# Batch 0's tokens loaded flat and its attention in two token halves: a cross-attention and snake-MLP kernel on one Trainium2 core, its first 312 steps in a new order

## The chip, the core and the metric

The kernel runs on one core of a Trainium2 chip. TensorE (PE) multiplies a stationary operand (loaded by LDWEIGHTS, PEld in the profile) with a moving one into the eight banks of PSUM; VectorE (DVE), ScalarE (ACT) and GpSimd (POOL) do the elementwise work, and SyncE (SP), ACT and POOL issue transfers (DMA). The metric is the device time of one execution in microseconds (us); less is better.

## The reference, cut to what matters

```python
# x: (8, 8, 512, 64), state: (8, 8, 32, 64); batch, head, token or slot, width
scores = scale * x @ state^T;   a = softmax(scores);    xread = a @ state
scores2 = scale * state @ x^T;  a2 = softmax(scores2);  sread = a2 @ x
rows = concat([xread, sread], axis=2)      # heads side by side: (8 * 544, 512)
h = rows @ w_in                            # w_in: (512, 2048)
g = h + sin(alpha * h) ** 2 / (alpha + 1e-9)
out = g @ w_out                            # w_out: (2048, 512), out: (4352, 512)
```

## The kernel before, in words

Work goes by tiles t = 0 to 7, one for each batch (its 512 tokens), and t = 8, the 256 state rows of all batches. For a batch the steps are, by the names of the methods:

- x is loaded (`lx`: a POOL transfer that casts to bf16; batch 0 instead `lq`: four transfers of SP, two heads each, in fp32), packed and cast (`pk`, for batch 0 `xq` on ACT), transposed (`xt`, for batch 0 `xtq`, on TensorE; from batch 2 on `td`, a transposing DMA of SP), and copied out of PSUM (`xc`).
- `sc`, `ex`, `rs`, `rr`, `nm`: scores against the transposed state `stT`, exponentials, sums over 32 slots, reciprocals, normalized weights A. The index after the batch is the group of four heads; each call covers all 512 tokens.
- A is transposed (`at` and `ac` on TensorE and a copy for batch 0; `ad`, a transposing DMA, for the others).
- `m` multiplies state with a quarter (slice s) of w_in, `me` evicts it to M. So h = A times M, and xread is never formed.
- `h` or `hg`: one block f of 128 of the 2048 columns of h, two products of 512 columns. `si`: sin(alpha h) on ACT. `sq`: the square, on the engine that the step names (A, V or G). `gt`: g, transposed, on VectorE.
- `o.t.st.f0.f1`: products f0 to f1 - 1 of the 16 that make the output tile of 128 rows; `oc` evicts it, `os` stores it.
- `w`, `cs`, `rc`, `xs`: sread of a batch, for tile 8. For batch 0 they come some 10 us after the last store of its tile.

The state of batches 0 and 1 comes early by `l_s01`, `s01_c`, `s01_t`, `s01_k`; that of the other batches by `l_st`, `st_t`, `st_c`. `li` and `lo` load a quarter of w_in and w_out each, 1 MB of fp32 cast to 0.5 MB, on POOL's queue. `l_alpha`, `al_t`, `al_c`, `inva` prepare alpha. `exp_table` and `sin_table` load ACT's function tables. `warm_up.n.cols.bank` is n products on zeros, whose result nobody reads.

Nothing is scheduled at run time: `ORDER` is a list of steps written out by hand or by a planner, and each engine executes its share of it strictly in this order; a step waits for its inputs and for its PSUM bank (the number in the step), and what stands behind it on its engine waits with it.

```python
    for step in ORDER:
        name, *args = step.split(".")
        getattr(steps, name)(*(int(a) if a.isdigit() else a for a in args))
```

Of the kernel before, what the change touches and what calls it, by code (L numbers as in the profile page):

```python
# [33 lines left out]
me.1.1.1.A warm_up.2.128.2 gt.0.2 si.0.0 warm_up.2.128.2 warm_up.2.128.6 warm_up.2.128.3
warm_up.2.128.2 warm_up.2.128.6 me.0.1.0.A gt.0.1 sq.0.0.G m.0.2.3.2 si.0.3 m.1.2.5.6 hg.0.4.0.7
me.0.2.0.V me.0.2.1.A hg.0.4.1 sq.0.3.G hg.0.6.0.4 me.1.2.1.V hg.0.6.1 si.0.4 hg.0.7.0.3 hg.0.11.0.2
me.1.2.0.V si.0.6 hg.0.7.1 sq.0.4.G hg.0.5.0.6 gt.0.0 hg.0.5.1 si.0.7 hg.0.11.1 hg.0.8.0.5 hg.0.8.1
sq.0.6.A gt.0.3 sq.0.7.G o.0.3.0.2.0 si.0.5 gt.0.4 o.0.3.2.3 o.0.0.0.2.1 si.0.11 o.0.0.2.3 gt.0.6
sq.0.5.G o.0.0.3.4 o.0.2.0.1.7 si.0.8 o.0.3.3.5 sq.0.11.A gt.0.7 hg.0.9.0.4 sq.0.8.G o.0.2.1.2
gt.0.5 o.0.2.2.4 hg.0.9.1 gt.0.11 o.0.0.4.5 hg.0.10.0.3 si.0.9 o.0.2.4.5 gt.0.8 o.0.0.5.6 o.0.3.5.6  # L40
sq.0.9.A o.0.3.6.8 pk.1.0.V hg.0.10.1 xt.1.1.6 pk.1.1.V si.0.10 gt.0.9 xt.1.0.2 xc.1.1.0.A sq.0.10.G
o.0.2.5.6 xc.1.1.1.V xc.1.0.0.A o.0.0.6.7 xc.1.0.1.V o.0.0.7.8 o.0.2.6.7 sc.1.1.5 gt.0.10 sc.1.0.4
m.0.3.6.2 ex.1.0 o.0.2.7.8 me.0.3.0.V o.0.1.0.3.3 me.0.3.1.V o.0.1.3.6 hg.0.13.0.6 o.0.1.6.7 ex.1.1
rs.1.0 hg.0.13.1 m.1.3.2.4 si.0.13 o.0.1.7.8 rr.1.0 rs.1.1 nm.1.0.0.4.G o.0.1.8.9 hg.0.12.0.5
o.0.3.8.9 rr.1.1 hg.0.12.1 me.1.3.0.V o.0.0.8.9 nm.1.1.0.4.G o.0.1.9.10 o.0.0.9.10 me.1.3.1.V
# [618 lines left out]
```

The softmax here doesn't subtract the row's maximum and nothing guards it: scores larger than these inputs give would overflow.

## Time and profile before

| | |
|---|---|
| median of 3 runs | 221.26 us (220.95 to 222.09) |
| the profiled execution: span from first to last instruction | 221.2 us; the profile gives no time beside it |
| PE, DVE, ACT, POOL busy | 97%, 73%, 78%, 48% of the span |
| instructions of PE and its share in the chain that ended last | 1619, 93% |
| warm-up products (line 303) | 66, 9.9 us, the last at 19.2 us |
| DMA queues: q0 (POOL), q1 (SP) | 8.13 MB and 15.08 MB, 26.1% of 16 engines each |
| first sine, first product of `o`, product of step o.1.1.0.1 | 16.52, 22.55, 45.85 us |

A line of the timeline is: start, length, engine, line of the code, operation, what it writes and reads, and how many are merged; in brackets the idle time of the engine before it and what ended it. The chain is followed back from the last instruction: at each step to what released it. "Busy" for PE counts matmuls that wait in its pipeline too, so neighbouring matmuls overlap in it.

### The profile page before, as it was taken

How to read it: one execution, taken by the hardware profiler on the slowest of the kernel's cores; microseconds unless marked ns; L12 is line 12 of the kernel's file. 1: busy time of each engine (PE TensorE's matmuls, PEld its weight loads, DVE VectorE, ACT ScalarE, POOL GpSimd, SP SyncE). 2: the span in 40 equal slices, each digit the busy share in tenths (PEclk: the TensorE clock that was granted, in tenths of full speed). 3: DMA queues.
4: the chain of work that ended last, by engine and by line, in shares of the span. 5: the costliest groups of instructions: out<-in, count | busy, mean ns of one | idle time of the engine just before them, and what ended most of it. 6: DMA issues, size and time to landing. Idle time of an engine off the chain costs nothing.

```text
span 221.2 us, 4330 instructions
## 1 busy us (share of the span) xinstructions
PE 215.7 (97%) x1619; PEld 106.0 (48%) x1619; DVE 162.4 (73%) x286; ACT 173.5 (78%) x297; POOL 107.1 (48%) x115
## 2 busy tenths in 40 slices
PE   7999999999999999999999999999999999999994
PEld 3664454444444444444454444445445555665452
DVE  3468986999678979988888778889766988571201
ACT  3589878998899979998996999798857897685111
POOL 6866626595388728934863377363501072121000
PEclk9999999999999999999999999999999999999999
DMA  6999995953549518375325437380220211012042
GB/s 172 198 206 204 205 203 87 174 199 73 119 127 158 96 50 150 44 190 61 81 41 125 126 95 94 108 117 17 47 99 0 98 47 47 0 50 95 1 142 96
DMA packets 38052, 23.48 MB, mean 106 GB/s; under 512 B 20992, under 2 KB 33680, under 8 KB 38032
## 3 DMA queue, kind: packets, MB, share of 16 engines
q0 software_dynamic: 11648, 8.13, 26.1%
q1 hardware_dynamic: 26128, 15.08, 26.1%
q8 instruction: 12, 0.20, 0.4%
q14 instruction: 8, 0.07, 0.1%
q10 hardware_dynamic: 256, 0.01, 0.1%
HBM read 17.44 MB, written 8.91 MB: 119 GB/s over the span
## 4 chain that ended last, share of the span: by engine, by line
PE 93%; ACT 3%; DMA 2%; SPq 0%; issue 0%
PE o_ps L587 54%; PE h_ps L537 22%; PE m_ps L488 4%; PE h_ps L543 3%; PE h_ps L552 3%; DMA x<-in_x_dram 2%; PE s_ps L399 2%; PE warm_ps L303 2%; PE w_ps L450 2%; PE w_ps L461 1%; PE x_ps L361 1%; ACT L226 1%; ACT s L560 1%; ACT M L496 1%; PE x_ps L376 0%; PE st_ps L333 0%
## 5 line engine op out<-in xcount | busy, mean ns | idle before, releaser
L587 PE MATMUL o_ps<-w_out_sb,gT 128*128 128x512 bf16 (+2 forms) x560 | 137.7, 373 | 0.0
L576 DVE SCALAR_TENSOR_TENSOR gT<-s,inva_sb,h_ps 128x512 bf16<-128x512 bf16 (+1 forms) x144 | 96.6, 714 | 18.8 <-POOL s L201 9.6
L201 POOL TENSOR_TENSOR s<-s 128x512 bf16<-128x512 bf16 (+1 forms) x76 | 76.7, 1021 | 65.9 <-ACT s L560 62.4
L560 ACT ACTIVATE s<-h_ps,alpha_sb 128x512 bf16<-128x512 f32 (+1 forms) x144 | 88.8, 671 | 10.5 <-PE h_ps L543 4.3
L587 PEld LDWEIGHTS <-gT 128*128 128x128 bf16 x560 | 52.3, 98 | 60.3 <-issue 5.0
L537 PE MATMUL h_ps<-AT,M 128*128 128x512 bf16 x224 | 60.8, 379 | 0.0
L537 PEld LDWEIGHTS <-M 128*128 128x128 bf16 x224 | 21.7, 98 | 25.9 <-issue 0.4
L569 ACT ACTIVATE s<-s 128x512 bf16<-128x512 bf16 (+1 forms) x53 | 31.4, 595 | 0.8
L201 POOL TENSOR_TENSOR A<-E,rR 128x512 bf16<-128x512 bf16 x16 | 16.6, 1048 | 25.7 <-ACT o_sb L595 12.7
L595 ACT COPY o_sb<-o_ps 128x512 f32<-128x512 f32 (+2 forms) x24 | 13.7, 571 | 16.6 <-PE o_ps L587 16.5
L496 ACT CAST M<-m_ps 128x512 bf16<-128x512 f32 x35 | 18.6, 594 | 8.2 <-PE m_ps L488 8.1
L496 DVE CAST M<-m_ps 128x512 bf16<-128x512 f32 x29 | 18.9, 679 | 2.5 <-PE m_ps L488 2.1
L595 DVE COPY o_sb<-o_ps 128x512 f32<-128x512 f32 x11 | 7.6, 691 | 13.0 <-PE o_ps L587 12.9
L303 PE MATMUL warm_ps<-warm 128*128 128x128 bf16 (+3 forms) x66 | 9.9, 295 | 1.4 <-DVE warm L209 1.2
L410 DVE TENSOR_REDUCE R<-E 128x16 f32<-128x512 bf16 x16 | 10.4, 658 | 1.1 <-ACT E L406 0.9
L201 DVE TENSOR_TENSOR s<-s 128x512 bf16<-128x512 bf16 (+1 forms) x15 | 6.2, 415 | 6.8 <-ACT s L560 6.7
L488 PE MATMUL m_ps<-w_in_sb,stT 64*32 64x512 bf16 x256 | 10.2, 382 | 0.0
L468 DVE RECIPROCAL rC<-w_ps 128x128 f32<-128x128 f32 x8 | 7.6, 948 | 3.2 <-PE w_ps L461 3.2
L406 ACT ACTIVATE E<-s_ps 128x512 bf16<-128x512 f32 x16 | 8.8, 601 | 1.4 <-PE s_ps L399 1.3
L552 PE MATMUL h_ps<-AT,M 128*128 128x512 bf16 x32 | 9.4, 380 | 0.4 <-ACT M L496 0.4
L543 PE MATMUL h_ps<-xs_all,w_in_sb 128*128 128x256 bf16 x64 | 9.1, 273 | 0.0
L560 ACT ACT_TABLE_LOAD x5 | 6.4, 1283 | 2.2 <-PE h_ps L537 1.1
(56 smaller groups left out, 104.3 us busy)
## 6 DMA issues: line engine op xcount, KB each, us to landing
out_dram<-o_sb SPq DMA_DIRECT2D x33, 256.0 KB, 2.3
xnat<-in_x_dram POOLq DMA_DIRECT2D x7, 512.0 KB, 7.7
w_in_sb<-in_moe_w_in_dram POOLq DMA_DIRECT2D x4, 512.0 KB, 10.3
w_out_sb<-in_moe_w_out_dram POOLq DMA_DIRECT2D x4, 512.0 KB, 16.3
x<-in_x_dram SPq DMA_DIRECT2D x4, 256.0 KB, 4.3
st_nat<-in_state_dram POOLq DMA_DIRECT2D x1, 256.0 KB, 5.7
out_dram<-o_sb SPq DMA_DIRECT2D x1, 192.0 KB, 1.9
s<-in_state_dram SPq DMA_DIRECT2D x1, 128.0 KB, 2.1
```

What stands on the lines that cost most here:

```text
L201: {"V": k.nc.vector, "G": k.nc.gpsimd}[eng].tensor_tensor(out, a, b, ALU.mult)
L303: k.nc.tensor.matmul(wp[:, :cols], k.warm[:, 0:k.P], k.warm[:, :cols], start=True, stop=True)
L488: k.nc.tensor.matmul(k.t["m", b, s + n, g][o0:o0 + k.Ns, :], k.stT[k.half(r), b * k.G + g, c0:c0 + k.Ns], k.w_in_sb[k.half(r), 2 * g + h, ...
L496: k.copy(eng)(k.t["M", b][:, g, s * k.FW:(s + 1) * k.FW], k.t["m", b, s, g][:])
L537: k.nc.tensor.matmul(hp[:, :n], k.t["M", t][:, g, fs], k.t["AT", t][:, g, :], start=(g == 0), stop=(g == k.G - 1),)
L543: k.nc.tensor.matmul(hp[:, :n], k.w_in_sb[:, q, fs], k.xs_all[:, q].rearrange("p b j -> p (b j)"), start=(q == 0), stop=(q == k.Q - 1),)
L552: k.nc.tensor.matmul(k.t["h", t, f][:], k.t["M", t][:, g, f * k.P:(f + 1) * k.P], k.t["AT", t][:, g, :], start=(g == 0), stop=(g == k.G - 1),)
L560: k.nc.scalar.activation(s[:, :n], k.t["h", t, f][:, :n], ACT.Sin, scale=k.alpha_sb[:, f:f + 1])
L569: k.nc.scalar.activation(s2[:, :n], s[:, :n], ACT.Square)
L576: k.nc.vector.scalar_tensor_tensor(gT[:, :n], k.t["s2", t, f][:, :n], k.inva_sb[:, f:f + 1], k.t["h", t, f][:, :n], ALU.mult, ALU.add,)
L587: k.nc.tensor.matmul(k.t["o", t, st, half][:, cols], k.t["gT", t, f][:, rows], k.w_out_sb[:, f, cols], start=(f == 0), stop=(f == k.FT - 1),)
L595: k.copy(eng)(o_sb[:, cols], k.t["o", t, st, half][:, cols])
```

## The change

- Batch 0's x is read flat: partition p holds 32 successive tokens of one head (2048 values). Columns j = 0 to 15 of the 32 come by two SP transfers in fp32 (`lf`) and two casts on ACT (`xn`), j = 16 to 31 by one casting POOL transfer (`lfb`). `lq`, `xq` and `xtq` go.
- `xth` transposes four pairs of columns j at a time, `xc` puts the result into `xT0` with the tokens of a half together. `sc0`, `ex0`, `rs0`, `rr0`, `nm`, `at0`, `ac0` do the attention of 256 tokens at a time. `sc0` takes one head at a time (32 moving columns, 64 rows), against a copy of the state, `st0T` (`s01_0`).
- `hh` does a block of h of tile 0 in two halves of 256 columns.
- The token-major x that `w.0` needs is now made by `td.0`, a transposing DMA of `xT0`; `w.0` has 32 products of 32 columns instead of 16 of 64.
- `os` of tile 0 writes its rows in the new token order, still 2 KB each.
- The first 312 steps have a new order: x of batch 0, then `li`, `lo`, `lx.1` and `l_st` in another order on POOL's queue, fewer warm-ups (13 products), other banks. From `o.1.1.0.1` on the steps are the same in the same order; only bank numbers differ.

The head of the list, old and new:

```diff
-touch_x l_s01 consts touch lq.0.S ident_ l_alpha lq.1.S zero.0 warm_up.7.512.3 exp_table lq.2.S
-zero.1 identf.V lq.3.S s01_c.G l_st li.0 xq.0.A s01_t.4 li.1 xtq.0.5 warm_up.1.384.3 xq.1.A
-s01_k.1.V s01_k.0.A li.2 xtq.1.6 warm_up.2.448.3 xc.0.0.0.V xq.2.A xc.0.0.1.V lo.0 al_t.7 xq.3.A
-xtq.2.0 warm_up.1.384.3 al_c inva sc.0.0.1 lo.1 xc.0.1.0.A warm_up.1.256.3 xtq.3.2 warm_up.2.128.3
-ex.0.0 warm_up.2.128.4 lx.1.0.1 warm_up.2.128.5 xc.0.1.1.V warm_up.2.128.6 warm_up.2.128.7 rs.0.0
-sc.0.1.0 li.3 st_t.0.3 ex.0.1 rr.0.0 st_t.1.4 lo.2 st_c.0.0.V st_c.0.1.A warm_up.2.128.5
-warm_up.2.128.6 warm_up.2.128.1 st_c.1.0.A rs.0.1 warm_up.2.128.2 warm_up.2.128.7 nm.0.0.0.4.G
-warm_up.2.128.0 warm_up.2.128.5 st_c.1.1.A warm_up.2.128.3 warm_up.2.128.6 warm_up.2.128.1 rr.0.1
-warm_up.2.128.2 sin_table warm_up.2.128.7 warm_up.2.128.0 nm.0.1.0.4.G at.0.0.5 warm_up.2.128.3
-ac.0.0.V m.0.0.6.4 m.1.0.1.2 lo.3 at.0.1.7 me.0.0.0.V me.0.0.1.A warm_up.2.128.0 warm_up.2.128.3
-me.1.0.1.A ac.0.1.V hg.0.2.0.5 me.1.0.0.V hg.0.1.0.4 hg.0.2.1 hg.0.1.1 hg.0.0.0.0 lx.2.0.1 si.0.2
-hg.0.0.1 m.1.1.6.3 si.0.1 m.0.1.7.2 hg.0.3.0.1 me.0.1.1.A sq.0.2.V hg.0.3.1 sq.0.1.G me.1.1.0.V
-me.1.1.1.A warm_up.2.128.2 gt.0.2 si.0.0 warm_up.2.128.2 warm_up.2.128.6 warm_up.2.128.3
-warm_up.2.128.2 warm_up.2.128.6 me.0.1.0.A gt.0.1 sq.0.0.G m.0.2.3.2 si.0.3 m.1.2.5.6 hg.0.4.0.7
-me.0.2.0.V me.0.2.1.A hg.0.4.1 sq.0.3.G hg.0.6.0.4 me.1.2.1.V hg.0.6.1 si.0.4 hg.0.7.0.3 hg.0.11.0.2
-me.1.2.0.V si.0.6 hg.0.7.1 sq.0.4.G hg.0.5.0.6 gt.0.0 hg.0.5.1 si.0.7 hg.0.11.1 hg.0.8.0.5 hg.0.8.1
-sq.0.6.A gt.0.3 sq.0.7.G o.0.3.0.2.0 si.0.5 gt.0.4 o.0.3.2.3 o.0.0.0.2.1 si.0.11 o.0.0.2.3 gt.0.6
-sq.0.5.G o.0.0.3.4 o.0.2.0.1.7 si.0.8 o.0.3.3.5 sq.0.11.A gt.0.7 hg.0.9.0.4 sq.0.8.G o.0.2.1.2
-gt.0.5 o.0.2.2.4 hg.0.9.1 gt.0.11 o.0.0.4.5 hg.0.10.0.3 si.0.9 o.0.2.4.5 gt.0.8 o.0.0.5.6 o.0.3.5.6
-sq.0.9.A o.0.3.6.8 pk.1.0.V hg.0.10.1 xt.1.1.6 pk.1.1.V si.0.10 gt.0.9 xt.1.0.2 xc.1.1.0.A sq.0.10.G
-o.0.2.5.6 xc.1.1.1.V xc.1.0.0.A o.0.0.6.7 xc.1.0.1.V o.0.0.7.8 o.0.2.6.7 sc.1.1.5 gt.0.10 sc.1.0.4
-m.0.3.6.2 ex.1.0 o.0.2.7.8 me.0.3.0.V o.0.1.0.3.3 me.0.3.1.V o.0.1.3.6 hg.0.13.0.6 o.0.1.6.7 ex.1.1
-rs.1.0 hg.0.13.1 m.1.3.2.4 si.0.13 o.0.1.7.8 rr.1.0 rs.1.1 nm.1.0.0.4.G o.0.1.8.9 hg.0.12.0.5
-o.0.3.8.9 rr.1.1 hg.0.12.1 me.1.3.0.V o.0.0.8.9 nm.1.1.0.4.G o.0.1.9.10 o.0.0.9.10 me.1.3.1.V
-si.0.12 o.0.0.10.11 o.0.3.9.11 sq.0.13.G ad.1 hg.0.15.0.2 sq.0.12.A o.0.1.10.12 hg.0.15.1 gt.0.12
-o.0.2.8.10 si.0.15 o.0.2.10.11 gt.0.13 o.0.0.11.12 hg.0.14.0.4 sq.0.15.A hg.0.14.1 o.0.3.11.13
...
+l_s01 ident_ touch_x consts lf.0.S touch zero.0 lfb lf.1.S l_alpha identf.V li.0 zero.1 exp_table
+li.1 s01_c.V warm_up.4.512.6 s01_t.0 lo.0 xn.0.A al_t.1 s01_0.V lx.1.0.1 s01_k.1.V s01_k.0.A
+warm_up.1.224.7 xth.0.0.2 xn.1.A al_c inva li.2 xc.0.0.A warm_up.1.352.0 xth.0.1.3 xth.0.2.4 lo.1
+xc.0.1.A xth.0.3.5 xc.0.2.V l_st sc0.0.6.7 xc.0.3.A ex0.0.0 warm_up.1.352.4 sc0.1.0.1 ex0.0.1 rs0.0
+ex0.1.0 ex0.1.1 sin_table rr0.0 warm_up.5.512.6 m.1.0.2.3 rs0.1 nm.0.0.0.2.G m.0.0.4.5 nm.0.1.0.2.G
+rr0.1 nm.0.0.2.4.V nm.0.1.2.4.G warm_up.1.512.1 at0.0.6 me.0.0.0.A m.0.1.7.0 li.3 ac0.0.V me.0.0.1.A
+at0.1.1 m.1.1.4.6 me.0.1.1.A ac0.1.V lo.2 hh.0.0.0.5 me.0.1.0.V me.1.0.1.A hh.0.0.1 hh.0.1.0.1
+hh.0.1.1 lo.3 me.1.0.0.V si.0.0 hh.0.2.0.0 hh.0.2.1 si.0.1 me.1.1.0.V hh.0.3.0.7 sq.0.0.G hh.0.3.1
+hh.0.4.0.3 si.0.2 me.1.1.1.V hh.0.4.1 hh.0.5.0.2 hh.0.5.1 si.0.3 sq.0.1.V sq.0.2.G gt.0.0 hh.0.6.0.4
+si.0.4 hh.0.6.1 gt.0.1 hh.0.7.0.6 si.0.5 sq.0.3.G hh.0.7.1 o.0.0.0.1.5 si.0.6 gt.0.2 xt.1.1.1
+sq.0.4.G si.0.7 gt.0.3 o.0.0.1.2 xt.1.0.0 xc.1.1.0.A xc.1.1.1.V sq.0.5.G sq.0.6.A o.0.1.0.1.7 gt.0.4
+sc.1.1.1 xc.1.0.0.A o.0.1.1.2 xc.1.0.1.V o.0.0.2.3 sq.0.7.G ex.1.1 o.0.2.0.1.3 gt.0.5 sc.1.0.0
+o.0.2.1.2 o.0.1.2.3 gt.0.6 o.0.3.0.1.2 o.0.3.1.2 o.0.2.2.3 gt.0.7 o.0.3.2.3 lx.2.0.1 o.0.0.3.4
+ex.1.0 m.0.2.4.1 pk.1.0.V o.0.1.3.4 pk.1.1.V me.0.2.0.A m.1.2.6.0 me.0.2.1.V o.0.2.3.4 me.1.2.1.A
+o.0.3.3.4 o.0.0.4.5 rs.1.0 me.1.2.0.A hh.0.8.0.4 hh.0.8.1 rs.1.1 st_t.0.1 si.0.8 rr.1.0 st_t.1.0
+rr.1.1 st_c.0.0.V nm.1.0.0.4.G hh.0.9.0.6 st_c.0.1.V hh.0.9.1 o.0.1.4.5 o.0.2.4.5 st_c.1.0.V
+nm.1.1.0.4.G si.0.9 hh.0.10.0.1 hh.0.10.1 sq.0.8.V o.0.3.4.5 st_c.1.1.A o.0.0.5.6 sq.0.9.V o.0.1.5.6
+si.0.10 ad.1 gt.0.8 o.0.2.5.6 hh.0.11.0.0 hh.0.11.1 gt.0.9 o.0.3.5.6 sq.0.10.G si.0.11 o.0.0.6.7
+o.0.1.6.7 o.0.2.6.7 m.0.3.4.6 sq.0.11.A gt.0.10 o.0.3.6.7 o.0.0.7.8 me.0.3.0.A o.0.1.7.8 gt.0.11
+o.0.2.7.8 me.0.3.1.A o.0.3.7.8 m.1.3.1.4 hh.0.12.0.0 me.1.3.0.A me.1.3.1.V hh.0.12.1 hh.0.13.0.6
...
```

The new and changed functions:

```diff
-    def lq(k, q, eng):
...
+    def flat(k):
+
+        return k.x[0].rearrange("h (b j) d -> (h b) j d", j=32)
+    def flat_sb(k):
+        return k.new(0, "xf", k.const, [k.P, 32, k.D], BF16)
+    def lf(k, part, eng):
+        k.t["xa", part] = k.const.tile([k.P, 8, k.D], FP32, name=f"xa_{part}")
         {"A": k.nc.scalar, "S": k.nc.sync}[eng].dma_start(
+            k.t["xa", part][:], k.flat()[:, 8 * part:8 * part + 8, :]
+        )
+    def lfb(k):
+        k.nc.gpsimd.dma_start(k.flat_sb()[:, 16:32, :], k.flat()[:, 16:32, :])
+    def xn(k, part, eng):
+        k.copy(eng)(k.flat_sb()[:, 8 * part:8 * part + 8, :], k.t["xa", part][:])
...
+    def xth(k, b, part, bank):
+        tp = k.t["xth", b, part] = k.ps(bank, [k.P, 4, k.P], BF16, "x_ps")
+        for m in range(4):
+            j = 8 * part + 2 * m
+            k.nc.tensor.transpose(
+                tp[:, m, :], k.flat_sb()[:, j:j + 2, :].rearrange("p j d -> p (j d)"), k.ident[:]
+            )
+    def xT0(k):
+
+        return k.new(0, "xT0", k.const, [k.P, 2, k.H, 8, 16], BF16)
...
     def td(k, b):
+        if b == 0:
+            xp = k.new(0, "xp", k.xppool, [k.P, 2, k.H, 2, k.D], BF16)
+            k.nc.sync.dma_start_transpose(
+                xp[:].rearrange("p e h r d -> p (e h) (r d)"),
+                k.xT0()[:].rearrange("p e h m t -> p (e h m t)"),
+            )
+            return
...
+    def sc0(k, half, *banks):
+
+        for r in range(2):
+            sp = k.t["sc0", half, r] = k.ps(banks[r], [k.P, k.H, k.Ns], FP32, "s_ps")
+        for h in range(k.H):
+            for r in range(2):
+                k.nc.tensor.matmul(
+                    k.t["sc0", half, r][:, h, :],
+                    k.xT0()[k.half(r), half, h].rearrange("d m t -> d (m t)"),
+                    k.st0T[k.half(r), h, :],
+                    start=True, stop=True,
+                )
+    def ex0(k, half, r):
+        E = k.new(0, "E", k.epool, [k.P, k.G, k.C, k.P], BF16)
+        k.nc.scalar.activation(
+            E[:, :, 2 * half + r, :],
+            k.t["sc0", half, r][:].rearrange("p (g h) j -> p g (h j)", g=2),
+            ACT.Exp, scale=k.scale,
+        )
...
+    def at0(k, half, bank):
+        tp = k.t["at0", half] = k.ps(bank, [k.P, k.G, 2, k.P], BF16, "a_ps")
+        for i in range(2):
+            for g in range(k.G):
+                k.nc.tensor.transpose(tp[:, g, i, :], k.t["A", 0][:, g, 2 * half + i], k.ident[:])
...
+    def hh(k, t, f, half, *bank):
+
+        if bank:
+            k.t["h", t, f] = k.ps(bank[0], [k.P, k.S], FP32, "h_ps")
+        c = slice(256 * half, 256 * half + 256)
+        for g in range(k.G):
+            k.nc.tensor.matmul(
+                k.t["h", t, f][:, c], k.t["M", t][:, g, f * k.P:(f + 1) * k.P],
+                k.t["AT", t][:, g, c], start=(g == 0), stop=(g == k.G - 1),
+            )
...
     def w(k, b, bank):
...
+        if b == 0:
+            for h in range(k.H):
+                for i in range(k.C):
+                    r, c = h % 2, h % 4 * k.Ns
+                    k.nc.tensor.matmul(
+                        wc[k.half(r), h // 2, r * k.Ns:(r + 1) * k.Ns],
+                        k.t["xp", 0][:, i // 2, h, i % 2, :], E[:, h // 4, i, c:c + k.Ns],
+                        start=(i == 0), stop=(i == k.C - 1),
+                    )
+            return
...
     def os(k, t, st, half=None):
...
+        if t == 0:
+            ov = k.out[0:k.S].rearrange("(b e m r) c -> e r m b c", b=16, e=2, m=8)
+            k.nc.sync.dma_start(ov[st // 2, st % 2][:, :, cols], o_sb[:, cols])
```

## The prediction

> **What bounds the kernel now.** I read the engines' shares and the forty slices first, then the chain that ended last, in order of time, then the timeline of the first 46 us.
>
> ```profile
> PE 215.7 (97%) x1619; PEld 106.0 (48%) x1619; DVE 162.4 (73%) x286; ACT 173.5 (78%) x297; POOL 107.1 (48%) x115
> ...
> PE   7999999999999999999999999999999999999994
> ...
> PEclk9999999999999999999999999999999999999999
> ```
>
> TensorE is the bound, but part of its head is padding: 66 warm-up products (line 303) fill the waits. From the chain, in order of time (start, length, what):
>
> ```profile
> 1.66 4.10 DMA x<-in_x_dram
> ...
> 13.73 1.28 ACT L226
> ...
> 22.71 2.16 PE o_ps L587 x10
> ```
>
> Batch 0 runs in series: load, cast, transposes, scores, exponentials, then the load of the sine table (1.28 us, over at 15.0), only then the evictions of M and the first sines. The timeline shows the two ends I count between:
>
> ```profile
> 9.74 1.08 PE L303 MATMUL warm_ps<-warm 128*128 128x128 bf16 x10
> ...
> 10.66 0.40 PE L399 MATMUL s_ps<-stT,xT 128*128 128x64 bf16 x8
> ...
> 12.01 1.62 PE L303 MATMUL warm_ps<-warm 128*128 128x128 bf16 x26
> ...
> 16.52 1.26 ACT L560 ACTIVATE s<-h_ps,alpha_sb 128x512 bf16<-128x512 f32 x2 [0.19 <-PE h_ps L552]
> ...
> 22.55 2.32 PE L587 MATMUL o_ps<-w_out_sb,gT 128*128 128x512 bf16 x10
> ...
> 45.85 0.38 PE L587 MATMUL o_ps<-w_out_sb,gT 128*128 128x512 bf16 x1
> ```
>
> The first sine is at 16.52, the first output product at 22.55. The product at 45.85 is step o.1.1.0.1: after it both lists hold the same steps in the same order, only with other PSUM banks. So the change is worth the shift of this moment, and what differs in cost behind it. Between 22.55 and 45.85 lie 23.3 us; the work there is 64 output products and 32 h products (six blocks of batch 0, ten of batch 1) at 0.2155 (a run of 17 spans 3.83 with the last one's 0.38), 20.7, and 64-row work (two m slices 0.34 each, x transposes 1.0, scores 0.57): 22.95. Only 0.35 us is idle, so before, everything after 22.55 is dense.
>
> **The head, step by step.** Cross-engine hand-offs are 0.03 to 0.1 us in the rows. The state load ends at 2.9 as now; the two remaining fp32 quarters of x are first on SP, so the second lands between 4.34 (the first quarter's today) and 5.76 (the second's); I take 5.76, the same place in the queue. The other half comes by a POOL load of 512 KB read and cast, issued at about 1.35, when the identity is built. Bounds: 4.1 us to landing (the shortest x quarter) and 5.7 (st_nat, the same shape and cast, with x in front), so 5.45 to 7.05; I take 6.9, near the row of the same shape. By the Trainium skill's "DMA: Bandwidth & Descriptors", Anatomy of one DMA (2.0 us plus bytes over 436 GB/s), it would land after 3.2 us, near 4.6; st_nat's own row is 2.5 us above that figure, and with 4.6 the first scores would wait for the quarter alone, a sum unchanged to 0.1.
>
> Alpha's transpose now stands ahead of the x transposes on TensorE and waits for its load (1.67 + 3.5 = 5.17); the cast of the second quarter ends later (5.78 + 0.62 = 6.4), so it hides. Four transposes (0.61) and a copy (0.59) make 7.7. The two transposes of the POOL half stand between, eight products at the slow 0.107, 0.86, done at 7.75: the halves are not independent, TensorE's queue makes the first scores wait for the second half's load. Sixteen score products per half: the slow row has 8 in 0.43 with the same weights, so 0.86: 7.75 to 8.6, and after a warm-up of 0.3 the second half to 9.75. Four exponentials of 256 columns (0.42 to 0.47 by the 256-column rows of lines 569 and 560, pitch 0.3) end at 10.6. The sine table follows at once, 1.28 + 0.2: done at 12.05 instead of 15.2. This is the gain's source: l_st, its 32 transposes (1.0) and three stT copies of ACT (0.47 each) have left this stretch.
>
> Sums 0.66, reciprocal 0.25 and two half normalizations on POOL (0.61, the 256-column row) give 11.8, then four transposes and the 0.42 copy 12.9; the second half's copy ends at 13.45. M's first evictions: 12.05 + 0.48 + 0.6 = 13.15. So h begins at 13.3 (before: 15.1, in earnest 15.9), 32 products of 256 columns at 0.108, 3.45 as before, and the first sine at 14.1. VectorE does four evictions (pitch 0.605) after 13.45, a square 0.42 and the first gT 0.74: 17.1; with 0.18 from gT to product (22.37 to 22.55 in the trace) the first output product starts at 17.25, 5.3 us earlier.
>
> **What it gives back.** At 17.25 only eight blocks of h are done, not ten, and st_t and two m slices are still to come: 64 output products 13.8, eight h blocks 3.45, ten of batch 1 4.3, four m slices 1.35, x transposes and scores 1.6, st_t 1.0: 25.5. And it is not dense. The first gT come at POOL's 1.04 to 1.08 per square, six of the eight on POOL, while every bank that the x transposes, scores and new output tiles take is freed by a gT. Stalls, put together from these rows: 0.45 before xt.1.1 (bank of block 1), 0.65 before the scores of batch 1 (VectorE's copy waits for ACT's, which stands behind eight sines at 0.6 pitch), 0.5 for the banks of blocks 4 and 5, 0.4 around m, st_t and stT copies, 0.3 at the meeting, where four output evictions now come together: 2.3. Meeting at 17.25 + 25.5 + 2.3 = 45.05: 0.8 earlier.
>
> The loads: 0.52 MB less stands ahead of w_in (x's half in bf16, st_nat later), 2.6 us at the 200 GB/s of the slices, so w_in's first slice lands at 9.0 instead of 11.6 (3.99 + 7.6) and lx.1, at 24.4 today, passes two more slices of 2.6 each and lands near 16.6, before the first output product; li.1 (some 11.6), li.2 (19.2), lo.1 (21.8) and st_nat (23.1), by the same 2.6 us a slice, are each half a microsecond or more ahead of their first use. Behind the meeting: td.0, one more SP transpose after ad.1, is needed only by w.0 at 56 and hides; its cover gone, it would cost its landing, 4.3. os.0 writes rows of the same 2 KB: nothing. w.0 has 32 products of half width for 16: at most 32 at 0.0316 (the 32 transposes of line 376 in 1.0 us) less today's 0.47, plus 0.54; at least 0 if the two column halves ran together; I take 0.45, near the transposes, which also alternate halves. It lies in the dense part and counts in full. The Trainium skill, "TensorE: Matmul & The Clock Gate", Back-to-back issue gap, speaks against this edit too: start-to-start never below about 25 ns however few columns, which would make it 0.33. No row shows 32 columns.
>
> Sum: 0.45 − 0.8 = −0.35 us. The profiled execution's span is 221.2, the median of the runs 221.26, so the runs hold nothing beside the span; 221.26 − 0.35 = 220.9. I count a change below 0.5% (1.1 us) as none.
>
> **Rivals.** Slower, by TensorE's clock. The profile's PEclk row is all nines, but the rows show two speeds: 512-column warm-ups take 0.42 each from 1.19, and 0.2155 later; the 128-column ones go from 0.1 to 0.056 at about 10. Before, warm-ups kept it busy from 6.46 on without a gap, and it was fast 3.5 us later; now 13 of 66 remain, and the time up to 9.75 holds small products and waits. Place: the five warm-ups and two m slices before the first evictions. If the busy stretch counts only from the end of those waits and the slow speed lasts one more such time, to 13.4, they take 2.13 + 1.24, m ends at 13.3 instead of 12.05: +1.25, 222.1. If it lasts through the h blocks, twice 3.45 against eight sines of 0.6 adds about 1.6: 223.7. It turns slower than my bound when the change of speed comes after about 13.5; I put it at 222.7. The same page, Part 1, says that about 3.4 us of sustained activity open the gate, in a window that runs freely of the kernel's start; estimated from that figure, the change could fall anywhere from 10 to 13.4 here. For it: the 75% busy stretch from 3.2 to 6.6 did not open it before. Against: from 6.5 to 13 TensorE hardly waits.
>
> Faster, by stalls that do not come. Loads at their early ends move the head by 0.5, and if ACT's and POOL's hand-offs let half of the 2.3 us vanish (before shows 0.35 of idle in its own stretch), 1.15 more: 219.2 to 220.1, say 219.6. Against: POOL was 4.70 of 5 us busy from 20 to 25 with the same six squares. It decides if the first sine is before 13.7.
>
> Third, the halves buy nothing: the second half's load, which stands ahead of the first scores in TensorE's queue, lands as late as st_nat did (8.95). Then scores start 2 us later, at most 1 of it is covered: 221.9, still no change by my bound.
>
> **Chances.** No change, the forecast and the third rival together, 0.43 (own range 220.2 to 222.2); faster 0.27; slower 0.30. The range, 219.2 to 223.2, takes in the faster case to its lower end and the clock rival past its middle; outside it, some 2 in 10 in all, lie a gain of both kinds in full and a slow clock through all of h.
>
> **What would show it.** Sine table over at 12.05, first sine 14.1, first output product 17.25, o.1.1.0.1 at 45.05; TensorE idle in 17 to 24 about 2 us and next to none from there on; w.0 at 0.9. Wrong, if 512-column products still take 0.42 after 11 us, if w_out or lx.1 are named as what TensorE waited for, or if idle time shows after 46 us.

## The result: slower by 3.2%

| | before | after |
|---|---|---|
| median of the runs beside each other | 221.44 us (220.95 to 222.09) | 228.37 us (227.71 to 229.94) |
| ratio, with its 95% interval | | 1.0323 (1.0278 to 1.0368) |
| span of the profiled execution | 221.2 us | 226.8 us |

The prediction was 220.9 us, "no change", in a range of 219.2 to 223.2. The time came out 7.5 us above it and 5.2 above the range.

A first thing to read is beside the profile: the execution of after whose span is 226.8 us took 228.84, and in all 33 later runs of before the time is the span and 1.8 to 1.9 us (runs of the changed kernels: mostly 1.9 to 2.2, once 2.9). I will come back to it. Of the four runs of after, the two with a mean granted clock of 0.99 took 228.84 (the profiled one) and 229.94 us, the two at 1.00 took 227.71 and 227.90.

The page of after, its engines and slices (each digit of a row is a fortieth of the span):

```profile
PE 212.5 (94%) x1603; PEld 105.6 (47%) x1630; DVE 163.5 (72%) x289; ACT 173.5 (77%) x298; POOL 106.0 (47%) x115
...
PE   4898995999999979999999999999999999999994
...
PEclk9999998899999999999999999999999999999999
```

TensorE was 97% busy and is now 94%. The row of 9s has holes at 34 to 40 us (5) and at 79 to 85 us (7), and at and behind the first of them, from 34 to 45 us, the granted clock is no longer 9. The chain of waits of after up to 60 us, in order of time (start, length, what):

```profile
2.92 9.91 DMA w_in_sb<-in_moe_w_in_dram
...
14.54 4.73 ACT s L663 x8
...
25.95 2.06 POOL A L200 x2
28.02 9.47 DMA AT<-A
37.54 0.61 PE h_ps L655 x2
```

The link that was not there before is `28.02 9.47 DMA AT<-A`: ad.1, the transposing DMA of batch 1's attention, 9.5 us to its landing, against 3.2 before. The timeline shows who paid, and when the meeting came (the steps that the prediction counted):

```profile
14.54 0.69 ACT L663 ACTIVATE s<-h_ps,alpha_sb 128x512 bf16<-128x512 f32 x1
...
17.51 0.39 PE L690 MATMUL o_ps<-w_out_sb,gT 128*128 128x512 bf16 x1
...
28.02 1.34 SPq L533 DMA_TRANSPOSE AT<-A  x1
29.49 7.65 SPq L417 DMA_TRANSPOSE xp<-xT  x1
37.54 0.61 PE L655 MATMUL h_ps<-AT,M 128*128 128x512 bf16 x2 [2.69 <-DMA AT<-A]
38.31 5.62 SPq L423 DMA_TRANSPOSE xT<-xp  x1
49.68 0.38 PE L690 MATMUL o_ps<-w_out_sb,gT 128*128 128x512 bf16 x1 [0.35 <-DVE o_sb L698]
82.54 0.64 PE L492 MATMUL s_ps<-stT,xT 128*128 128x64 bf16 x16 [1.26 <-DMA xT<-xp]
```

The first sine (14.54) and the first output product (17.51) are where the prediction put them (14.1, 17.25). The meeting, o.1.1.0.1, is not: 49.68, not 45.05. And there is idle time behind it, 1.26 us for the xT of td.4, where the prediction said next to none. The windows show what followed the wait (per row: window, its length, busy time of PE, PEld, DVE, ACT, POOL, granted clock, DMA share, GB/s):

```profile
36.00:38.00 2.00, 0.46 (x3) 0.23 (x4) 1.87 (x5) 0.00 (x0) 0.00 (x0) 1.00 1.46 136
38.00:40.00 2.00, 2.00 (x7) 0.78 (x6) 0.29 (x1) 0.69 (x1) 0.69 (x1) 0.56 1.34 182
40.00:42.00 2.00, 2.00 (x7) 0.70 (x6) 0.75 (x1) 1.30 (x2) 1.39 (x2) 0.59 1.29 113
42.00:44.00 2.00, 2.00 (x11) 0.89 (x10) 1.90 (x4) 1.79 (x4) 0.00 (x0) 1.00 1.39 142
```

From 38 to 42 the clock is at 0.56 to 0.59: seven products in 2 us instead of eleven. The 13 products from 37.54 to 42.04 took 4.5 us where 13 times 0.2155 is 2.8: 1.7 us more, on top of the wait of 2.7. The windows of 2 us blur the edges: the granted clock is 0.50 from 38.24 to 41.65 us and full on either side.

### The profile page after: what moved, and what is told of

It reads as the page before. It is cut to its first block, busy times and chain, and to the rows that moved or that the text cites. A ratio compares the mean times of both kernels' runs of the same rounds, so it can differ in the third digit from the quotient of the medians.

```text
span 226.8 us, 4336 instructions
## 1 busy us (share of the span) xinstructions
PE 212.5 (94%) x1603; PEld 105.6 (47%) x1630; DVE 163.5 (72%) x289; ACT 173.5 (77%) x298; POOL 106.0 (47%) x115
## 4 chain that ended last, share of the span: by engine, by line
PE 79%; DMA 11%; DVE 3%; ACT 2%; POOL 2%; issue 1%; POOLq 0%
PE o_ps L690 47%; PE h_ps L640 19%; DMA w_in_sb<-in_moe_w_in_dram 4%; DMA AT<-A 4%; PE m_ps L591 3%; PE h_ps L646 3%; DMA xT<-xp 3%; PE h_ps L655 2%; ACT s L663 2%; PE w_ps L553 1%; PE s_ps L492 1%; PE w_ps L564 1%; DVE gT L679 1%; POOL A L200 1%; DVE R L503 1%
## 5 line engine op out<-in xcount | busy, mean ns | idle before, releaser
L690 PE MATMUL o_ps<-w_out_sb,gT 128*128 128x512 bf16 (+2 forms) x537 | 134.6, 375 | 2.0 <-issue 0.9
L640 PE MATMUL h_ps<-AT,M 128*128 128x512 bf16 x201 | 54.9, 379 | 0.2
L640 PEld LDWEIGHTS <-M 128*128 128x128 bf16 x204 | 19.8, 98 | 23.9 <-issue 1.0
L200 POOL TENSOR_TENSOR A<-E,rR 128x512 bf16<-128x512 bf16 (+1 forms) x17 | 16.4, 980 | 29.7 <-ACT o_sb L698 14.8
L672 ACT ACTIVATE s<-s 128x512 bf16<-128x512 bf16 (+1 forms) x50 | 29.3, 589 | 0.8
L599 ACT CAST M<-m_ps 128x512 bf16<-128x512 f32 x39 | 20.7, 592 | 9.3 <-PE m_ps L591 9.0
L599 DVE CAST M<-m_ps 128x512 bf16<-128x512 f32 x25 | 16.2, 680 | 2.5 <-PE m_ps L591 2.4
L698 DVE COPY o_sb<-o_ps 128x512 f32<-128x512 f32 x11 | 7.5, 688 | 13.9 <-PE o_ps L690 13.8
L200 DVE TENSOR_TENSOR s<-s 128x512 bf16<-128x512 bf16 (+1 forms) x19 | 8.4, 447 | 6.8 <-ACT s L663 6.8
L655 PE MATMUL h_ps<-AT,M 128*128 128x512 bf16 x20 | 6.9, 433 | 2.7 <-DMA AT<-A 2.7
L482 PE MATMUL h_ps<-AT,M 128*128 128x256 bf16 x64 | 8.0, 273 | 0.0
L646 PEld LDWEIGHTS <-w_in_sb 128*128 128x128 bf16 x64 | 6.3, 98 | 3.4
```

Source lines behind the costliest of these rows:

```text
L200: {"V": k.nc.vector, "G": k.nc.gpsimd}[eng].tensor_tensor(out, a, b, ALU.mult)
L599: k.copy(eng)(k.t["M", b][:, g, s * k.FW:(s + 1) * k.FW], k.t["m", b, s, g][:])
L640: k.nc.tensor.matmul(hp[:, :n], k.t["M", t][:, g, fs], k.t["AT", t][:, g, :], start=(g == 0), stop=(g == k.G - 1),)
L646: k.nc.tensor.matmul(hp[:, :n], k.w_in_sb[:, q, fs], k.xs_all[:, q].rearrange("p b j -> p (b j)"), start=(q == 0), stop=(q == k.Q - 1),)
L655: k.nc.tensor.matmul(k.t["h", t, f][:], k.t["M", t][:, g, f * k.P:(f + 1) * k.P], k.t["AT", t][:, g, :], start=bool(bank), stop=not bank,)
L672: k.nc.scalar.activation(s2[:, :n], s[:, :n], ACT.Square)
```

## Experiments

The theories, by their letters: **L**, the loads on POOL's queue slow ad.1, which is now issued while they still run; **Q**, td.0, queued on SP right behind ad.1, takes its share; **C**, the clock is slow because the start has few warm-ups; **H**, POOL's early loads make the head's own loads late; **R**, the new order of steps is the loss and the new head gains nothing. The ratios are to runs of before on the same chip.

### What slows ad.1

**e1: td.0 later** (behind tile 0's stores).

```diff
-si.0.15 td.0 o.0.3.8.9
+si.0.15 o.0.3.8.9
-os.0.3 h.1.8.7
+os.0.3 td.0 h.1.8.7
```

> The changed kernel with td.0 moved from behind ad.1 to behind the four stores of tile 0 on SP's queue. Theory L (the loads on POOL's queue, which fill the DMA engines until about 36 us, slow the transposing DMA ad.1, 9.5 us to landing against 3.1 before): AT still lands 8 to 9.5 us after its issue, TensorE still waits over 2 us at hg.1.0, time within 1 us of the changed kernel's 228.4. Theory Q (ad.1 is slow because the twice as large td.0 follows it 1.5 us later on the same queue and shares its rings): AT lands within 3 to 5.5 us, the wait at hg.1.0 is gone, time 223 to 225. Theory C (the loss is TensorE's slow clock from too few warm-ups, the rival of the prediction): nothing changes.

230.37 us, 1.0402 (1.0348 to 1.0455). AT landed after 7.2 us and TensorE was idle only 0.4 there, at full clock; but here ad.1 was issued at 30.92, the head being late, so it landed no earlier than in after (38.1 against 37.5). In its new place td.0 is late itself: TensorE waits 0.5 for it, and 2.3 for the xT of td.3 and td.4 behind it. The stall moved, it did not go.

**e2: A.1 transposed on TensorE**, ad.1 removed, td.0 left in place.

> The changed kernel with A of batch 1 transposed by TensorE (at.1, ac.1 in two free banks, eight products more, 0.46 us, and two copies of VectorE) in place of ad.1; td.0 stays. Theories L and Q: no wait and no slow clock at 35 to 42 us, o.1.1.0.1 at 45.3 to 46.3 us instead of 49.7, time 223.5 to 225 if what is lost behind that point (some 1.7 us of span) stays. Theory C: the wait goes, but a slow stretch remains, time above 226.

231.93 us, 1.0448 (1.0399 to 1.0497): a flaw of the experiment. With ad.1 gone, td.0 is the first on SP and runs at once (`11.10 7.06 SPq L418 DMA_TRANSPOSE xp<-xT  x1`), in the midst of the loads; lx.1 then lands at 22.7 instead of 18.3, so that TensorE waits 2.5 us for it. A transposing DMA among the loads costs the loads, too.

**f2: td.0 right behind td.2**, and **f3: the same with A.1 on TensorE.**

> The changed kernel with td.0 right behind td.2 on SP instead of right behind ad.1. Theory Q (td.0 on the queue behind ad.1 takes part of its engines' time): ad.1 lands after about 7.2 us instead of 9.5, TensorE waits 0.4 to 0.9 for it instead of 2.7, the granted clock stays full, td.2 lands in time, and td.0 lands before 52, so that no later wait for xp or xT is left: 228.4 - 2.3 (wait) - 0.9 (slow stretch, in half of the runs) - 1.2 (wait for td.4's xT) = 224.0 (223 to 225). Theory L alone (the loads slow ad.1 whoever stands behind it): ad.1 still takes 9 us and more, TensorE waits 2.5, 227 to 228.

> As the run before it, and ad.1 is replaced by eight transposes on TensorE and two copies of VectorE (at.1, ac.1), so that no transposing DMA stands in the loads at all. Theories L and Q: no wait for AT is left, the clock stays full; the transposes add 0.5 us of TensorE and the copies 0.85 of VectorE: 223.5 (222.5 to 225). Rival V (VectorE, 0.97 busy from 14 to 30, becomes the bound): the copies push gT back, TensorE waits for gT and o copies 1.5 to 2 us instead: 225 to 226.5.

f2: 227.88 us, 1.0287 (1.0227 to 1.0347). Its timeline:

```profile
29.34 1.34 SPq L533 DMA_TRANSPOSE AT<-A  x1
38.38 0.61 PE L655 MATMUL h_ps<-AT,M 128*128 128x512 bf16 x2 [2.21 <-DMA AT<-A]
39.41 2.76 SPq L423 DMA_TRANSPOSE xT<-xp  x1
```

Nothing is behind ad.1 for 10 us, and it still lands 9.0 us after its issue. Q falls. f3: 228.49 us, 1.0312 (1.0275 to 1.0348), without any wait for AT: my 223.5 is missed by 5, so ad.1 cannot be the whole loss either. The first blocks of h of tile 1 now wait for gT instead (1.35 and 0.72 us), and this execution's first output product is late (19.04; 17.51 in after).

**f4: fewer loads in flight**, ad.1 and td.0 where the change puts them: lo.2 and lo.3 are left out, every output product uses the first half of w_out in their place (the output's values change), and lx.3 moves behind td.2.

```diff
-hh.0.1.1 lo.3 me.1.0.0.V
+hh.0.1.1 me.1.0.0.V
-                k.w_out_sb[:, f, cols], start=(f == 0), stop=(f == k.FT - 1),
+                k.w_out_sb[:, f % 8, cols], start=(f == 0), stop=(f == k.FT - 1),
```

> The changed kernel with fewer loads in flight under ad.1: slices 2 and 3 of w_out are not loaded (products f = 8 to 15 read slices 0 and 1 in their place), and lx.3 is issued behind td.2; ad.1 and td.0 stand where they are, one behind the other. Theory L (the loads share the DMA engines with ad.1): its landing falls from 9.5 us to 3.1 to 4, TensorE does not wait for AT, the clock stays full, o.1.1.0.1 at 45.5 to 46.5 instead of 49.68, time 222 to 224. Theory Q (td.0 behind it): the landing stays at 5.4 and more (3.1 + 2.3). If the landing stays near 9.5, neither loads nor their share of the engines slow it.

228.17 us in its one run, where I had expected 222 to 224; but the question was ad.1. Its timeline:

```profile
30.21 1.34 SPq L533 DMA_TRANSPOSE AT<-A  x1
31.68 2.08 SPq L417 DMA_TRANSPOSE xp<-xT  x1
...
36.87 0.59 PE L655 MATMUL h_ps<-AT,M 128*128 128x512 bf16 x2
```

The landing falls to 3.4 us with td.0 still right behind it, and TensorE does not wait. L holds. That the time does not follow has two parts: from its first output product to the meeting f4 is 3.2 us quicker than after (28.9 against 32.2), but its first output product is 2.2 us later (19.69), and behind the meeting it loses 0.4 more. The DMA view says how (packets, MB, share of 16 engines; q0 is POOL's queue, q1 SP's). After, from 28 to 30, from 30 to 32 and from 32 to 34 us:

```profile
q0 software_dynamic: 411, 0.41, 124.5%
...
q0 software_dynamic: 577, 0.40, 132.1%
q1 hardware_dynamic: 2, 0.00, 0.2%
...
q0 software_dynamic: 467, 0.24, 86.5%
q1 hardware_dynamic: 509, 0.13, 46.8%
```

f4, from 30 to 32 us:

```profile
q1 hardware_dynamic: 397, 0.10, 25.1%
q0 software_dynamic: 8, 0.00, 1.4%
```

In after, two of ad.1's packets move in the first 4 us after its issue; then it shares the engines with the rest of lo.3, with lx.2 and lx.3. By the Trainium skill, "DMA: Bandwidth & Descriptors", Queues, rings and completion order, each DMA engine takes turns between queues, a packet from each. From 32 to 34 us the counts are near that (509 to 467), from 34 to 36 us they are not (630 to 288); the silent start, some 2.5 us beyond the 1.34 of issue, does not fit it, and no run here explains it.

The kernel before issues its ad.1 at 32.9 us (f1 below) and at 35.0 (the profile shown), when the loads in front are just done or nearly so (in f1 q0 falls from 677 packets in 32 to 34 us to 108 in 34 to 36). AT landed at 36.6 and at 38.2. **In the new order ad.1 was issued at 28.0 to 30.9 and landed at 37.5 to 38.3** in five executions (after, e1, e3, f2, g1), and at 37.0 and 36.5 with lx.2 moved (g2, g3). The loads, not the issue, set its end.

**g2: lx.2 issued with ad.1 instead of 6.4 us ahead of it** (td.0 as in f2).

> The changed kernel with td.0 behind td.2, and lx.2 issued behind the normalization that releases ad.1 instead of 6 to 7 us ahead of it. Theory L: 512 KB (1 MB read, about 2.6 us of the loads' stream at 200 GB/s in bf16) less stand in front of ad.1, so AT lands near 35 to 35.7 instead of 37.5 to 38.3, TensorE waits 0 to 0.6 for it instead of 2.2; lx.2 lands near 38 and its pack may then be late by up to 1. Time 225.5 to 227 against 227.9 of the run with td.0 behind td.2 alone. If L is wrong, AT lands at 37.5 to 38.3 again and the time is 227.9 or more.

227.34 us, 1.028 (1.0207 to 1.0354). ad.1's packets start a window earlier, 502 of them in 30 to 32 us, but the last ones share the engines with lx.2 (258 in 34 to 36) and it lands at 37.0: 9.4 us. My 35 to 35.7 missed: I had counted what stands in front, and not what runs beside.

### What the wait does to the clock

**e3: twelve 512-column warm-ups ahead of the first block of tile 1** (`warm_up.12.512.0` before `hg.1.0.0.0`), nothing else.

> The changed kernel with twelve warm-up products of 512 columns (2.6 us) put ahead of hg.1.0, into the wait for AT. Theories L and Q: AT lands as before, at 37 to 38 us; the clock stays at full speed through 38 to 42 us, which is worth the half of the 3.4 us at 0.5 that fell on real products, so 1.3 to 2 us: time 226.3 to 227.2. If the slow clock cost nothing because ACT, POOL or VectorE set the pace there: 228.4 as the changed kernel.

226.11 us, 1.0214 (1.0169 to 1.026): 2.3 us less than after, by doing useless work. The windows answer to those of after above:

```profile
36.00:38.00 2.00, 1.78 (x9) 0.69 (x8) 2.00 (x5) 0.00 (x0) 0.00 (x0) 1.00 1.48 127
38.00:40.00 2.00, 2.00 (x10) 0.88 (x9) 0.29 (x1) 1.08 (x2) 0.34 (x1) 1.00 1.35 182
```

AT landed after 9.6 us, as in after, but the clock is full, ten products in 2 us. The meeting is at 48.4, 1.3 earlier: the slow clock's 1.7, less 0.3 by which AT landed later. The other 1.3 is td.4's xT, in time in this profile. Beside the two runs of after at full clock (227.71 and 227.90) the gain is 1.7.

**When the clock falls.** In every profile here the granted clock changes only at multiples of 3.41 us from the moment at which it is first recorded as full: in after 10.93 us, then 38.24 (8 steps later) and 41.65 (9 steps). Of these steps, counted over all 18 profiles, the clock fell after every one in which TensorE was busy for less than 0.4 of the time (after, from 34.83 to 38.24 us: 0.71 of 3.41 us) and after none in which it was busy for half or more (f2, from 34.41 to 37.82: 1.75). So a wait of 2.2 to 2.7 us can cost nothing or 3.4 us at half the clock, by where it falls in the steps. In f2 it was split between two. By their mean clocks, only two of the four runs of after had this loss.

**C, at the start.** The profile's clock column says nothing of the time before that first moment; the products do. One line each of after and of e1:

```profile
10.71 0.93 PE L312 MATMUL warm_ps<-warm 128*128 128x512 bf16 x3 [0.22 <-issue]
...
11.72 2.32 PE L312 MATMUL warm_ps<-warm 128*128 128x512 bf16 x5
```

In after the products of 512 columns come every 0.2155 us from 10.9 on; in e1 the five warm-ups from 11.72 on still come every 0.427, and the clock is full at 15.5 only; 0.42 after 11 us was one of the prediction's signs of being wrong. Over the fourteen other profiles with the new head this moment lies between 9.5 (g2) and 15.5 us (e1), in those with before's head at 10.5 (shown), 5.8 (f1) and 5.6 (e5). From the first exponential to the first sine it is 5.1 us in after and g2, where the clock came early, and 5.9 to 6.2 in e1, e2, f2 and f4, where it came after 13.9. So C is not what slowed the stretch at 38 us, but it holds for the head, by up to 1.1 us in some executions. In after TensorE is idle for 2.3 us ahead of alpha's transpose at 6.24, a place where before had warm-ups and transposes; that this delays the clock is likely but not shown, since no run put warm-ups back there.

### What the profiled execution of before was worth

**f1: the kernel before, unchanged, profiled again.**

> The kernel before, unchanged, profiled once more, to see which base the sum should have had. Theory B (base): the profiled execution shown of before had a late head; runs of before have spans of 219.0 to 219.5 for times of 220.9 to 221.4 (1.9 us beside the span), so this profile has a span near 219.4, the first output product near 20.9 instead of 22.55, o.1.1.0.1 near 44.1 instead of 45.85, and the same rows from there on. Rival: the head is as in the profile shown (22.55 and 45.85) and the 1.8 us lie elsewhere, behind 46 us.

220.95 us, span 219.1. Its timeline:

```profile
7.97 0.60 ACT L406 ACTIVATE E<-s_ps 128x512 bf16<-128x512 f32 x1
...
11.54 1.28 ACT L226 ACT_TABLE_LOAD   x1
...
14.33 1.27 ACT L560 ACTIVATE s<-h_ps,alpha_sb 128x512 bf16<-128x512 f32 x2 [0.19 <-PE h_ps L552]
...
20.42 2.32 PE L587 MATMUL o_ps<-w_out_sb,gT 128*128 128x512 bf16 x10
...
43.72 0.38 PE L587 MATMUL o_ps<-w_out_sb,gT 128*128 128x512 bf16 x1
```

First sine 14.33 instead of 16.52, first output product 20.42 instead of 22.55, the meeting at 43.72 instead of 45.85. **The profile that the prediction worked from had a head 2.1 us late**; from its first output product on it is the same to 0.02 us. e5, another execution with before's head, has its first sine at 13.98. The late head goes with the late clock: full at 10.5 us in the profile shown, at 5.8 in f1.

**e5: before with lx.3 right behind lx.2**, to put loads beside its ad.1.

> The kernel before with the load lx.3 issued right behind lx.2 (about 16 us instead of 36), so that the loads end at about 37 instead of 34.6 us and ad.1, issued at 35.0, meets 2 us of them. Theory L: ad.1 needs 4.5 to 6 us to landing instead of 3.1 (its landing is at 38.2 now and its first use at 38.9), TensorE waits 0.5 to 2 us at h.1.2, time 222 to 224. Theory Q: no td.0 here, so no change (221 to 222).

224.41 us, 1.0123 (1.0053 to 1.0194). ad.1, issued at 34.87 and on the engines from 36.2, took 3.9 us, not more: by then the loads were nearly done (182 packets of q0 in 36 to 38 us). A weak test of L. The profiled execution took 222.93 us, so it shows only half of the extra 3 us of the median, and what it shows is not ad.1's: the moved load waits 3.3 us on POOL for earlier loads, and POOL's squares behind it wait too (TensorE: 1.85 us for a gT at 19.9).

### Whether the new head gains anything

**h1: the new head, and from the first block of h on the old order.** **h2** has the state's cast on POOL in addition.

> One half of the change alone: batch 0's flat load and its attention in halves up to M and AT of tile 0 as in the changed kernel, and from the first block of h on the steps of the kernel before in their old order (banks 1 and 4 exchanged, l_st's transposes st_t behind o.0.0.11.12, td.0 behind td.2). Theory R (the new head gains nothing on a usual run of before, whose first sine is at 14.33, and the loss is the new order: ad.1 at 28 us in the loads and what follows): first sine 14.5 to 15.5, the 32 transposes of st_t now in the dense part (+1.0), w.0 +0.2, ad.1 issued at 33.5 to 35, behind the loads, lands in 3.2 to 4.1 and nobody waits, the clock stays full, no wait for td.4: 221.3 + 0.6 + 1.0 + 0.2 = 223.1 (222.3 to 224.2). Rival 1 (the head is worth what the prediction gave it): 220.5 or less. Rival 2 (the flat load itself is the loss): 226 and more.

> As the run before it, with the state's cast on POOL between lfb and li.0, so that w_in does not stand beside the x quarters. Theory H: xa lands at 4.5 after its issue in every run, the head scatters less, 0.3 to 0.8 below the run before it: 222.6. Rival: w_in's first slice, 1.1 us later, is then what M waits for, no gain.

229.15 us, 1.0342 (1.029 to 1.0394), and 228.91, 1.032 (1.0274 to 1.0365): not a test of R, as one line of h1's timeline shows.

```profile
21.26 0.63 PE L589 MATMUL m_ps<-w_in_sb,stT 64*32 64x512 bf16 x16 [3.45 <-DMA w_in_sb<-in_moe_w_in_dram]
```

The old order wants w_in's third slice at 18, and the new load order has lx.1 and lo.0 ahead of it. The granted clock then is 0.50 for 3.4 us (22.31 to 25.73). The change's two orders, of loads and of steps, go only together.

**h3: as h1, with the loads in the old order too** (w_in 0, 1, 2, w_out 0, 1, lx.1, w_in 3, l_st); **h4** with the cast on POOL.

> The new head with the old order behind it, mended: in the run before, the third slice of w_in stood behind lx.1 and lo.0 on POOL's queue as in the changed kernel, and the old order, which needs it at 18, waited 3.4 us for it and then ran 3.7 us at half the clock. Here the loads stand in the old order (w_in 0, 1, 2, w_out 0, 1, lx.1, w_in 3, then l_st). Theory R (new order, not new head, is the loss): no wait for w_in, ad.1 issued at 34 to 36 and landing in 3 to 4, full clock: 223.1 (222.3 to 224.2). Rival 1 (the head is worth its forecast): 220.5 or less. Rival 2 (the flat load and the halves lose by themselves): 226 and more.

> As the run before it, with the state's cast on POOL between lfb and the first slice of w_in. Theory H: the head scatters less and is 0.3 to 0.8 earlier: 222.6. Rival: M waits for w_in's first slice, which comes 1.1 us later, no gain or 0.5 more.

h3: 224.84 us, 1.0148 (1.008 to 1.0215); h4: 224.63, 1.0138 (1.0077 to 1.02). h3's timeline:

```profile
21.30 1.90 PE L688 MATMUL o_ps<-w_out_sb,gT 128*128 128x512 bf16 x8
...
33.78 1.34 SPq L531 DMA_TRANSPOSE AT<-A  x1
...
41.18 0.39 PE L688 MATMUL o_ps<-w_out_sb,gT 128*128 128x512 bf16 x1 [0.68 <-DVE gT L677]
...
46.59 0.38 PE L688 MATMUL o_ps<-w_out_sb,gT 128*128 128x512 bf16 x1
```

Same order as f1, so each moment can be set beside f1's: the first output product 0.9 later (21.30 to 20.42), the meeting 2.9 later (46.59 to 43.72). In between lie st_t's 1.0, now in the dense stretch, and a stall of about 0.8 where I put it. ad.1, issued at 33.78, lands in 3.1 us and nobody waits. So in these two executions the new head by itself loses 0.9 and gains nothing (h4: 1.4), with the clock full at 12.6 us against f1's 5.8; in the medians, with st_t moved behind it, the loss is 3.3 in all. The other 3.6 of the 6.9 us come with the new orders of loads and steps, ad.1 in the loads among them; the runs don't divide them further. h3 is 0.6 above the range that I gave for R, and h4's cast brought nothing clear of noise, as its rival said. R holds for the head; "the loss is the new order" is only half true.

### Attempts at a better version

**g1: the state's cast on POOL**, so that w_in starts 1.1 us later. **g3: g2, g1 and lx.4 one normalization earlier. g4: f3 with g1 and the earlier lx.4.**

> The changed kernel with the cast of the early state (s01_c) on POOL between lfb and li.0, as the kernel before has it: POOL issues its first slice of w_in only when the state has landed, at about 3.3 us instead of 2.2, and the two x quarters of SP and alpha have less beside them. Theory H (the early loads of POOL make xa and alpha late: 4.9 to 6.9 us to landing against 3.2 for the first quarter of x before): xa lands by 5.3, alpha by 5.6, the sine table is over 0.7 to 1.5 us earlier than in the changed kernel (11.95), first output product near 16.8. Theory L (ad.1 can't run before the loads in front of it are done, at 37 to 38 us, whenever it is issued): the time hardly moves, 227.5 to 228.5, and TensorE's wait for AT grows by what the head gained. Rival to L: the head's gain arrives, 227.0 or less.

> The run before it, and the state's cast on POOL, and lx.4 issued one normalization (1.0 us) earlier so that td.4 comes earlier. H and L: the head's 0.7 to 1.5 us arrive in part now that AT is no longer held so long, and the wait of 1.3 us for td.4's xT goes: 223.5 to 225. Rival: each only uncovers the next wait (pack of lx.2, gT at the first blocks of tile 1): 226 to 227.

> A.1 transposed on TensorE and copied by VectorE (no ad.1), td.0 behind td.2, the state's cast on POOL, lx.4 one normalization earlier. With no transposing DMA in the loads the head's gain of 0.7 to 1.5 us arrives in full: 228.5 - 1.1 - 1.0 (td.4's xT) = 226.4 (225.5 to 227.2). Rival: the stalls for gT at the first blocks of tile 1 (1.4 and 0.9 us) are set by squares and gT and eat it: 227.5.

g1: 229.62 us, 1.0384 (1.0346 to 1.0422): xa landed after 4.5 us (4.9 in after), yet the first sine is at 15.31, with M waiting 0.35 for w_in; H's gain does not arrive. AT landed 9.4 us after its issue and TensorE waited 2.6 with the clock falling behind it, as L has it. g3: 226.99, 1.027 (1.0219 to 1.0321); g4: 227.04, 1.0277 (1.0225 to 1.0329). Both are a little below the changed kernel, neither near the kernel before, and g3 still waits 1.25 us for td.4's xT (g4: 0.47), so an earlier lx.4 does not cure it. g4 is inside the range that I gave it, g3 came out as its rival said. No version beat before.

## Why the prediction was wrong, step by step

Set the profiled executions of after and f1 side by side; the spans differ by 226.8 - 219.1 = 7.7 us:

| term | predicted | measured |
|---|---|---|
| first output product, against before | -5.3 | -2.9 (17.51 - 20.42) |
| TensorE's work from there to the meeting (25.5 - 22.95) | +2.55 | +2.55, not measured apart |
| idle or slow in that stretch, less before's 0.35 | +1.95 | +6.3 |
| of it the wait for AT | 0 | 2.7 |
| of it the slow clock behind the wait | 0 | 1.7 |
| of it all other stalls, less before's 0.35 | 1.95 | 1.9 |
| behind the meeting | +0.45 | +1.75 (177.1 - 175.4) |

**The base.** "The profiled execution's span is 221.2, the median of the runs 221.26, so the runs hold nothing beside the span" was the first failure. Every later run of before holds 1.8 to 1.9 us beside the span, so I estimate that this execution took about 223.1 and stood 1.8 above the median. The head was the late part, and the head was what the change replaced: I set a new head against an old one on a bad day. Of the gain of 5.3 us, 2.1 was that day. What is left, 2.9, is no faster head either: f1's first sine is at 14.33, after's at 14.54, and the first output product comes earlier because eight blocks of h stand ahead of it instead of ten, work that is paid back before the meeting.

**The head itself** was predicted well in its times: table load over at 12.15 (12.05), first sine 14.54 (14.1), first product 17.51 (17.25). That is partly luck. The two x loads landed 0.8 and 0.9 later than I had them (6.56 and 7.79), so that the first scores start at 8.80, not 7.75; and sixteen score products took 0.40 us, not 0.86, which wins it back. The exponentials start at 9.39, 1.4 later than f1's 7.97; between the first of them and the table load the halves save 2.3, and then M waits for the second slice of w_in, whose landing (12.83, from the chain) I had at 11.6. It is the same with the other loads of POOL's queue: w_in's first slice landed at 10.3 and not at 9.0, lx.1 at 18.3 and not at 16.6. Over the other profiles with this head the first sine lay between 14.07 and 17.43. The "gain's source" was 0.9 us of table load on a usual run, and none of it reached the first sine.

**ad.1** was the failed step of the mechanism. The working says that each queue that a step is moved past counts; I priced td.0 ("hides") and never asked what happens to ad.1 when it is issued at 28 instead of 35. Before's own windows had the answer in their DMA share: 1.38 from 32 to 34 us, 0.06 from 34 to 36, and its ad.1, issued at 35.0, landed in 3.2 us.

```profile
32.00:34.00 2.00, 2.00 (x17) 0.73 (x16) 1.93 (x5) 1.09 (x1) 1.06 (x2) 1.00 1.38 191
34.00:36.00 2.00, 2.00 (x11) 0.94 (x10) 0.76 (x2) 1.96 (x4) 2.00 (x3) 1.00 0.06 8
```

f4 shows the loads as the cause and f2 acquits td.0. With the clock it cost 4.4 us in the profiled run, where the sum had nothing.

**The stalls** I had put at 2.3 came to about that in sum, though not item by item: the 0.46 us ahead of the first x transposes was a wait for lx.1, one of the signs that I had named for being wrong, and not for a bank. f4 and f3 show that they do not fall when ad.1's wait is gone: the stretch from the first output product to the meeting takes 28.9 and 31.0 us, and less the 25.5 of work (in f3 0.5 more for A's transposes) that leaves 3.4 and 5.0. The largest waits with a name in them are for gT.

**Behind the meeting**, w.0's 32 products took 0.64 us from the first start to the next product's in e3 (58.93 to 59.57) against 0.47 in f1: +0.17, not 0.45. Their own starts lie 17 ns apart on average (0.52 us over 31), below the floor of about 25 ns that the prediction quotes; the two column halves come in pairs some 5 ns apart. What I did not have is the wait for td.4's xT, 1.26 us: in after its landing takes 5.9 us, in f1 4.3. It appears in every profile of the changed order but e3's (0.47 to 1.64). Why it lands later was not settled.

**The rivals.** The clock rival had the right resource. In after's profile the start kept its place, the clock being full at 10.9, and the wait at 35 lost it; in e1, e2, f2, f4 and h4 the clock came after the 13.5 that the rival had named, so after's profile was a good one in this. "Halves buy nothing" was nearest for the head, for another reason than it gave.

## What to carry to other kernels

Before a new head is set against the profile's head, find out whether that execution was a usual one: compare its whole time, not its span, with the runs. When a change brings a DMA forward, look up in the DMA row what fills the engines at its new moment; a transfer that must wait for the loads lands when the loads end, however early it is issued. Before a stretch is made shorter, ask what it was waiting for besides itself: here lx.2 lands at 34.7 and 35.5 us in two profiles of before and at 37.5 in after, and what needed the DMA engines could not come sooner. When a stretch is judged by its time in one profile, look first when TensorE's clock was full in it.

## What the hardware showed that I had not expected

- A transposing DMA of 256 KB (ad.1) took 3.1 to 3.9 us to its landing with the loads done, 7.2 to 9.6 beside them, and in its first 4 us moved two packets (after).
- The granted clock fell to 0.50 for 3.41 us after idle stretches of 2.6 to 2.7 us (after, g1, g2) and of 3.1 and 3.5 (h2, h1); it stayed full after 2.2 (f2) and 2.5 (e2), where the stretch was split between two steps of 3.41 us. The Trainium skill, "TensorE: Matmul & The Clock Gate", Why this matters for your kernels, asks for no gaps over about 3 us: here less was enough, and the share of a step decided.
- VectorE's pack of batch 2 (two copies) took 0.76 us while POOL was idle (f2), and 1.64 (f4) and 2.21 (e1) beside two of POOL's squares.
